# The last layer's second product from float16 pairs, normalised ahead of the transposes

## The chip, the cores and the metric

The kernel runs on one core of one Trainium2 chip. The time of a run is the device time of that core in microseconds (us), and a kernel's time is the median of its runs. Inside the core five engines work beside each other, each through its own instructions in order: TensorE (PE in the profile, its weight loads PEld), VectorE (DVE), ScalarE (ACT), GpSimd (POOL) and SyncE (SP), which issues most of the DMAs. They wait for one another by semaphores.

## The reference, cut to what matters

Three layers follow one another on 2 x 768 = 1536 tokens of 512 features: a clustered attention, a mixture of eight experts of which each token takes one, and a feed-forward layer. The change lies in the last one (and in one load of the second):

```python
h = x @ w_in                                   # 1536x512 by 512x1024
h_max = np.max(h, axis=-1, keepdims=True)
e = np.exp(h - h_max)
sm = e / (np.sum(e, axis=-1, keepdims=True) + 1e-09)
solu = h * sm
mu = np.mean(solu, axis=-1, keepdims=True)
var = np.mean((solu - mu) ** 2, axis=-1, keepdims=True)
ln = (solu - mu) / np.sqrt(var + 1e-06) * g_ln
return (ln @ w_out).astype(np.float32)         # 1536x1024 by 1024x512
```

## The kernel before, in words

**Order of the work.** The order of all instructions is written out by hand. The attention follows the list FLAT. The experts and the preparation of the last layer's weights follow the list MOE (lines 96 to 118), whose steps have a letter and numbers: N and X read an expert's number and load its rows (X.3 those of place 3), W loads its weights, C and Q split a weight chunk (the difference on VectorE or on GpSimd), T transposes the rows, G and H are the expert's first and second product, S stores; P, J and R load and narrow the chunks of w_in (0 to 7) and w_out (8 to 15), K splits a chunk of w_in, M (`m2_gain`, line 1241) multiplies a chunk of w_out by g_ln on ScalarE. There are eight places, one for each expert, in order of their size. An engine works its own steps in the order of the list, so a step that waits holds up what stands behind it on that engine.

**Pairs.** A float32 product is made of three products of rounded values: each operand is split into a high part (rounded by ScalarE) and a low part (the difference, by VectorE or GpSimd), and `mm3` (lines 1036 to 1040) multiplies high by high, high by low and low by high into one PSUM bank. The parts are of type float32r.

**The last layer.** It goes by 12 tiles of 128 tokens, in a loop of 15 iterations (the last lines of `body`). In iteration t TensorE has the first product of tile t (`l_h`, 24 products of 512 columns), the eight transposes of tile t-2 (`l_trans`, line 1362) and the second product of tile t-3 (`l_out`, 24 products of 512 columns into the bank pf), in this order. `l_soft(t)` is the softmax part on VectorE and ScalarE: two maxima (line 1329), a one-column step that joins them (line 1330), two exponentials (line 1334), and u, the product of h and the exponentials (line 1340). `l_norm(t)` makes the mean and the variance of u with two statistics instructions and one that joins them (lines 1348 and 1349), subtracts the mean from u (line 1350, 1024 columns) and has GpSimd make the reciprocal deviation in five one-column steps (lines 1352 to 1356, the last a power). `l_norm(t-1)` stands inside `l_soft(t)`, ahead of u(t). The reciprocal deviation is used only when the finished tile leaves PSUM (line 1376). `l_trans` copies the transposed tile out of the PSUM tile pc, of which there is one, into the pair c: the high part by ScalarE (line 1364), the low part by VectorE (line 1365). GpSimd also makes the low parts of the x tiles from tile 2 on (`l_split`, line 1055) and, in iterations 0 to 2, behind the softmax, the low parts of w_out's eight chunks (line 1033); it issues the scatter of each finished tile (line 701).

That there is one transposed tile at a time, and two finished ones, is said here:

```python
ps_c = ctx.enter_context(tc.tile_pool(name="ps_c", bufs=1, space=PSUM))
ps_f = ctx.enter_context(tc.tile_pool(name="ps_f", bufs=2, space=PSUM))
```

Of the kernel before, what the change touches and what calls it, by code (L numbers as in the profile page):

```python
# [38 lines left out]
NWK = 15  # L39
# [62 lines left out]
W.2.5 C.2.5 W.2.6 G.2.2 E.9 G.2.1 C.2.10 H.2.0 N.3 C.2.9 W.2.7 R.7.0 C.2.8 H.2.1 X.3 P.9 C.2.14 W.3.0 G.2.3 R.7.1  # L102
# [11 lines left out]
X.7 G.6.1 C.6.11 Q.6.10 G.6.3 H.6.0 Q.6.12 W.7.1 Q.6.13 G.6.4 H.6.1 C.6.15 C.7.3 H.6.2 T.7.0 C.6.14 T.7.3 G.6.6 C.7.0  # L114
C.7.1 H.6.3 G.6.5 H.6.4 W.7.2 W.7.3 T.7.2 K.6 T.7.1 G.6.7 Z H.6.5 C.7.7 C.7.4 G.7.0 C.7.5 K.1 C.7.2 M.13 H.6.6 H.6.7
W.7.4 W.7.5 S.6 Q.7.6 M.9 G.7.1 K.0 Q.7.8 Q.7.9 G.7.2 O W.7.6 W.7.7 K.2 Q.7.15 C.7.10 M.12 H.7.0 H.7.1 H.7.2 M.8 G.7.3
C.7.13 Q.7.11 C.7.12 G.7.4 C.7.14 M.11 G.7.5 H.7.3 G.7.6 K.3 K.4 H.7.4 G.7.7 M.14 K.7 M.10 H.7.5 H.7.6 M.15 K.5 H.7.7
# [11 lines left out]
def body(ctx, tc, i, o):  # L129
# [895 lines left out]

    wk = ctx.enter_context(tc.tile_pool(name="wk", bufs=NWK))
# [212 lines left out]

    def m2_gain(c):  # L1240
        nc.scalar.activation(m2n[:, c, :], m2n[:, c, :], AF.Copy, scale=gln[:, c - 8 : c - 7])
# [10 lines left out]
    def last_banks():  # L1252
# [9 lines left out]
        "S": lambda k: wins[k].store(), "P": prep_load, "J": lambda c: prep_load(c, nc.gpsimd), "R": narrow, "E": lambda j: LATE[j](), "K": m2_split, "M": m2_gain,  # L1262
# [58 lines left out]
    def l_soft(t):  # L1321
# [15 lines left out]
        if 0 < t < T - 1:  # L1337
            l_norm(t - 1)
        for half in range(2):
            nc.vector.scalar_tensor_tensor(out=u[:, half], in0=h[:, half], scalar=sc, in1=e[:, half], op0=ALU.mult, op1=ALU.mult)  # L1340
        if t == T - 1:
            l_norm(t)

    def l_norm(t):
# [5 lines left out]
        nc.vector.tensor_scalar(u, u, sm[:, 4:5], None, op0=ALU.subtract)  # L1350

# [6 lines left out]
    def l_trans(t):  # L1358
# [4 lines left out]
        c = z["c"] = l2.tile([128, 2, 1024], F32R, tag="c2", name=f"c2_{t}")  # L1363
        nc.scalar.activation(c[:, 0], pc_, AF.Copy)
        nc.vector.tensor_tensor(out=c[:, 1], in0=pc_, in1=c[:, 0].bitcast(F32), op=ALU.subtract)  # L1365

    def l_out(t):
# [3 lines left out]
        for f in range(NF):  # L1371
            w = m2[8 + f]
            fs = slice(f * 128, f * 128 + 128)
            mm3(po, (c[:, 0, fs], c[:, 1, fs]), (w[:, 0], w[:, 1]), f == 0, f == NF - 1)
        ob = l2.tile([128, 512], F32, tag="ob", name=f"ob_{t}")
        nc.scalar.activation(ob, po, AF.Copy, scale=z["sm"][:, 6:7])
# [3 lines left out]
    for t in range(T + 3):  # L1380
        if 0 < t < T:
            l_h(t)
# [88 lines left out]
```

## Time and profile before

| | us |
|---|---|
| median of 3 runs (lowest, highest) | 582.01 (581.5, 583.67) |
| the profiled execution, its own time | 579.94 |
| its span, from the first to the last instruction | 578.1 |
| TensorE busy in the span | 547.7 (95%) |
| VectorE busy | 403.9 (70%) |
| ScalarE busy | 296.5 (51%) |
| GpSimd busy | 256.9 (44%) |

The granted clock of TensorE is 0.996 of full speed (2.4 GHz) in the mean of the span. Busy shares are averages over stages with different limits, and a busy TensorE is counted with the modelled ends of its products, so it is read by the starts of its instructions: the distance from one start to the next is what a product costs. In a timeline a row stands for one or several instructions of one line (the count behind x), with its start and its duration in front; the brackets at the end tell how long the engine idled before it and what ended that. A duration holds what the instruction waits for once it was begun.

### The profile page before, as it was taken

The numbers are of one execution on the slowest core, as the hardware profiler recorded it, in microseconds if no ns is written. First come the engines' busy times: TensorE is split into PE (matmuls) and PEld (weight loads), VectorE is DVE, ScalarE is ACT, GpSimd is POOL, SyncE is SP. The second block draws the span as 40 slices with busy tenths as digits, with TensorE's granted clock in tenths as the row PEclk, the third lists the DMA queues.
The fourth block names the chain that finished last, engine by engine and source line by source line (L and its number), as shares of the span: only waits on it lengthen the run. The fifth ranks groups of instructions, "written<-read, shape, count | busy, mean of one in ns | idle before, by whom it ended". The sixth has DMA issues, their size and how long they took to land. (4 is left out here: it accounts for less than half of the span.)

```text
span 578.1 us, 12327 instructions
## 1 busy us (share of the span) xinstructions
PE 547.7 (95%) x4652; PEld 469.4 (81%) x4654; DVE 403.9 (70%) x811; ACT 296.5 (51%) x635; POOL 256.9 (44%) x283
## 2 busy tenths in 40 slices
PE   6898899999999999899999999999999999999995
PEld 3676678777778877799999998989988788888884
DVE  6788888787988787748585699877547655544550
ACT  5765776766666565232232468677546424232230
POOL 7467777888675993410000101221307723333221
PEclk9999999999999998999999999999999999999999
DMA  7248468647332110999939577774000000001000
GB/s 256 83 113 261 122 176 255 177 112 226 74 84 59 42 53 19 322 339 394 382 125 385 163 254 252 218 249 152 33 3 2 18 19 18 19 18 39 18 37 36
DMA packets 28866, 81.06 MB, mean 140 GB/s; under 512 B 5356, under 2 KB 5868, under 8 KB 28804
## 3 DMA queue, kind: packets, MB, share of 16 engines
q1 hardware_dynamic: 26020, 70.80, 38.4%
q0 software_dynamic: 2784, 9.44, 4.5%
q8 instruction: 38, 0.62, 0.4%
q14 instruction: 24, 0.20, 0.1%
HBM read 56.17 MB, written 11.53 MB: 117 GB/s over the span
## 5 line engine op out<-in xcount | busy, mean ns | idle before, releaser
L556 POOL TENSOR_TENSOR pl<-pe 128x768 f16<-128x768 f32 (+1 forms) x97 | 128.8, 1347 | 54.6 <-ACT pe L548 48.3
L548 ACT ACTIVATE pe<-pS 128x384 f32<-128x384 f32 x192 | 89.4, 490 | 62.2 <-PE pS L539 54.9
L485 DVE TENSOR_REDUCE ohb<-pm 128x1 bf16<-128x768 f32 x77 | 73.4, 954 | 23.6 <-PE pm L483 23.3
L538 PE MATMUL pS<-w 81*128 81x384 f32 (+1 forms) x192 | 76.8, 400 | 1.9 <-ACT w L508 1.2
L539 PE MATMUL pS<-w 128*128 128x384 f32 x192 | 67.0, 349 | 0.0
L572 PE MATMUL pa<-v,pe 128*128 128x65 f16 x576 | 64.7, 196 | 0.0
L572 PEld LDWEIGHTS <-pe 128*128 128x128 bf16 x576 | 52.9, 98 | 13.9 <-issue 13.4
L573 PE MATMUL pa<-v,pe 128*128 128x64 f16 x576 | 64.0, 195 | 0.0
L574 PE MATMUL pa<-v,pl 128*128 128x65 f16 x576 | 63.7, 193 | 0.0
L573 PEld LDWEIGHTS <-pe 128*128 128x128 bf16 x576 | 54.0, 99 | 0.2
L574 PEld LDWEIGHTS <-pl 128*128 128x128 f16 x576 | 53.9, 99 | 0.0
L1033 POOL TENSOR_TENSOR wk<-rw,wk 128x512 fp32r<-128x512 f32 x13 | 17.7, 1369 | 72.7 <-ACT wk L1032 65.0
L483 PE MATMUL pm<-w 80*128 80x512 f32 (+1 forms) x154 | 43.8, 366 | 5.6 <-DVE ohb L485 3.2
L1334 ACT ACTIVATE e<-h,sm,smeta 128x512 f32<-128x512 f32 x24 | 18.5, 774 | 56.6 <-DVE sm L1330 56.6
L1329 DVE TENSOR_REDUCE sm<-h 128x1 f32<-128x512 f32 x24 | 15.4, 684 | 44.4 <-PE h L1040 41.5
L538 PEld LDWEIGHTS pS<-w 81*128 81x128 f32 (+1 forms) x192 | 37.6, 196 | 8.8 <-ACT pe L548 3.1
L1033 DVE TENSOR_TENSOR wk<-rw,wk 128x512 fp32r<-128x512 f32 x49 | 36.4, 761 | 7.4 <-ACT wk L1032 7.1
L1032 ACT ACTIVATE wk<-rw 128x512 fp32r<-128x512 f32 x62 | 36.7, 630 | 9.1 <-DMA rw<-in_w_dram 7.1
L1038 PE MATMUL pf<-m,c 128*128 128x512 f32 x96 | 38.8, 404 | 0.0
L539 PEld LDWEIGHTS pS<-w 128*128 128x128 f32 x192 | 38.1, 198 | 0.0
L1038 PE MATMUL h<-m,x 128*128 128x512 f32 x96 | 37.7, 392 | 0.4 <-PEq L1294 0.4
L1039 PE MATMUL pf<-m,c 128*128 128x512 f32 x96 | 37.9, 395 | 0.0
(290 smaller groups left out, 1448.9 us busy)
## 6 DMA issues: line engine op xcount, KB each, us to landing
rw<-in_w_dram SPq DMA_DIRECT2D x31, 512.0 KB, 4.4
wk<-in_w_dram SPq DMA_DIRECT2D x25, 512.0 KB, 8.0
w<-w SPq DMA_DIRECT2D x42, 192.0 KB, 4.0
xs_d<-zrow SPq DMA_DIRECT2D x8, 512.0 KB, 5.3
w_w<-in_w_dram SPq DMA_DIRECT2D x8, 512.0 KB, 7.0
raw<-in_qT_dram SPq DMA_DIRECT2D x8, 384.0 KB, 3.8
raw<-in_kT_dram SPq DMA_DIRECT2D x8, 384.0 KB, 4.8
vraw<-in_v_dram SPq DMA_DIRECT2D x8, 384.0 KB, 5.8
```

Source lines behind the costliest of these rows:

```text
L483: nc.tensor.matmul(pm[:, c0:c1], w[0:80, M0 + h, 0, t * 128 : t * 128 + 128], w[0:80, M0 + h, 1, c0:c1], start=True, stop=True)
L485: nc.vector.tensor_reduce(out=s["oh"][:, t, 0, h, C : C + 1], in_=pm, op=ALU.max, axis=AX.X)
L538: nc.tensor.matmul(pS, w[0:kr, M0 + h, 1, ts], w[0:kr, M0 + h, 0, c0:c1], start=b0 == 0, stop=False, skip_group_check=True)
L539: nc.tensor.matmul(pS, w[:, B0 + h, 1, ts], w[:, B0 + h, 0, c0:c1], start=False, stop=True, skip_group_check=True)
L548: nc.scalar.activation(pe[:, e0 - b0 : e0 + n], s["bank"][:, : kb * n], AF.Exp, scale=0.125)
L556: eng.tensor_tensor(out=pl, in0=pe, in1=ph, op=ALU.subtract)
L572: nc.tensor.matmul(pa[:, o0 : o0 + D + 1], ph[:, qs], vh, start=(t == 0 and qt == q0), stop=False, skip_group_check=True)
L573: nc.tensor.matmul(pa[:, o0 : o0 + D], ph[:, qs], vl, start=False, stop=False, skip_group_check=True)
L574: nc.tensor.matmul(pa[:, o0 : o0 + D + 1], pl[:, qs], vh, start=False, stop=(t == NT - 1), skip_group_check=True)
L1033: (eng or nc.vector).tensor_tensor(out=t[:, 1, :], in0=rw, in1=t[:, 0, :].bitcast(F32), op=ALU.subtract)
L1038: nc.tensor.matmul(out, a[0], b[0], start=first, stop=False, skip_group_check=True)
L1039: nc.tensor.matmul(out, a[0], b[1], start=False, stop=False, skip_group_check=True)
```

## The change

The second product of the last layer takes its operands as pairs of float16 in place of float32r (`out_split` and the new lines of `l_trans`). For that w_out times g_ln is scaled by a power of two that the chip finds: eight maxima (the new steps B on VectorE), two small steps that join them (Y, the second with a float32 product of 128 columns on TensorE), and the gain M now multiplies by g_ln times that scale and so stands behind Y in the list. The transposed activations are multiplied by 512, and what leaves PSUM by one constant (`osc`). The reciprocal deviation moves from there to the activations: `l_apply` subtracts the mean and multiplies by it, ahead of the transposes, and takes the place of the subtraction in `l_norm`. `l_norm(0)` moves to the end of `l_soft(0)`; `l_apply(t-1)` stands behind u(t), for tile 0 ahead of u(1). The splits of w_out's chunks 8 to 13 move ahead of the softmaxes of tiles 0 and 1. And X.3 stands two steps of SP's earlier, ahead of W.2.7.

```diff
-W.2.5 C.2.5 W.2.6 G.2.2 E.9 G.2.1 C.2.10 H.2.0 N.3 C.2.9 W.2.7 R.7.0 C.2.8 H.2.1 X.3 P.9 C.2.14 W.3.0 G.2.3 R.7.1
+W.2.5 C.2.5 W.2.6 G.2.2 E.9 G.2.1 C.2.10 H.2.0 N.3 X.3 C.2.9 W.2.7 R.7.0 C.2.8 H.2.1 P.9 C.2.14 W.3.0 G.2.3 R.7.1
...
-X.7 G.6.1 C.6.11 Q.6.10 G.6.3 H.6.0 Q.6.12 W.7.1 Q.6.13 G.6.4 H.6.1 C.6.15 C.7.3 H.6.2 T.7.0 C.6.14 T.7.3 G.6.6 C.7.0
-C.7.1 H.6.3 G.6.5 H.6.4 W.7.2 W.7.3 T.7.2 K.6 T.7.1 G.6.7 Z H.6.5 C.7.7 C.7.4 G.7.0 C.7.5 K.1 C.7.2 M.13 H.6.6 H.6.7
-W.7.4 W.7.5 S.6 Q.7.6 M.9 G.7.1 K.0 Q.7.8 Q.7.9 G.7.2 O W.7.6 W.7.7 K.2 Q.7.15 C.7.10 M.12 H.7.0 H.7.1 H.7.2 M.8 G.7.3
-C.7.13 Q.7.11 C.7.12 G.7.4 C.7.14 M.11 G.7.5 H.7.3 G.7.6 K.3 K.4 H.7.4 G.7.7 M.14 K.7 M.10 H.7.5 H.7.6 M.15 K.5 H.7.7
+X.7 G.6.1 C.6.11 Q.6.10 G.6.3 B.8 H.6.0 Q.6.12 W.7.1 Q.6.13 G.6.4 H.6.1 C.6.15 B.9 C.7.3 H.6.2 T.7.0 C.6.14 T.7.3
+G.6.6 C.7.0 B.10 C.7.1 H.6.3 G.6.5 H.6.4 W.7.2 W.7.3 T.7.2 B.11 K.6 T.7.1 G.6.7 Z H.6.5 C.7.7 C.7.4 B.12 G.7.0 C.7.5
+K.1 C.7.2 H.6.6 H.6.7 B.13 W.7.4 W.7.5 S.6 Q.7.6 G.7.1 K.0 B.14 Q.7.8 Q.7.9 G.7.2 O W.7.6 W.7.7 K.2 B.15 Q.7.15 C.7.10
+Y.0 H.7.0 H.7.1 H.7.2 G.7.3 C.7.13 Y.1 Q.7.11 C.7.12 M.13 G.7.4 C.7.14 M.9 G.7.5 H.7.3 M.12 G.7.6 K.3 M.8 K.4 H.7.4
+M.11 G.7.7 K.7 M.14 H.7.5 H.7.6 M.10 M.15 K.5 H.7.7
...
+    am2 = kp.tile([128, NF + 3], F32, name="am2")
+    gsc = kp.tile([128, NF], F32, name="gsc")
+    osc = am2[:, NF + 1 : NF + 3]
+
+    def m2_max(c):
+        nc.vector.tensor_reduce(out=am2[:, c - 8 : c - 7], in_=m2n[:, c, :], op=ALU.max, axis=AX.X, apply_absolute_value=True)
+
+    def m2_scale(part):
+        m = am2[:, NF : NF + 1]
+        if part == 0:
+            nc.vector.tensor_tensor(out=am2[:, :NF], in0=gln, in1=am2[:, :NF], op=ALU.mult)
+            nc.vector.tensor_reduce(out=m, in_=am2[:, :NF], op=ALU.max, axis=AX.X, apply_absolute_value=True)
+            return
+        px = PL.ps_t.tile([128, 512], F32, tag="pt", name="pt_scale")
+        nc.tensor.matmul(px[:, :128], m.to_broadcast([128, 128]), identf, start=True, stop=True)
+        nc.vector.tensor_reduce(out=osc[:, 0:1], in_=px[:, :128], op=ALU.max, axis=AX.X)
+        nc.vector.tensor_scalar(osc[:, 0:1], osc[:, 0:1], 2.0 ** -90, None, op0=ALU.max)
+        nc.vector.tensor_scalar(bits(osc[:, 0:1]), bits(osc[:, 0:1]), 0x7F800000, None, op0=ALU.bitwise_and)
+        nc.vector.tensor_scalar(bits(osc[:, 1:2]), bits(osc[:, 0:1]), -1.0, float(268 << 23), op0=ALU.mult, op1=ALU.add)
+        nc.vector.tensor_scalar(gsc, gln, osc[:, 1:2], None, op0=ALU.mult)
+        nc.vector.tensor_scalar(bits(osc[:, 0:1]), bits(osc[:, 0:1]), 1.0, float(-23 << 23), op0=ALU.mult, op1=ALU.add)
+
     def m2_gain(c):
-        nc.scalar.activation(m2n[:, c, :], m2n[:, c, :], AF.Copy, scale=gln[:, c - 8 : c - 7])
+        nc.scalar.activation(m2n[:, c, :], m2n[:, c, :], AF.Copy, scale=gsc[:, c - 8 : c - 7])
+
+    def out_split(c, pool):
+        t = pool.tile([128, 2, 512], F32R, tag="wk", name=f"m2_{c}")
+        hi, lo = (t[:, j].bitcast(F16)[:, :512] for j in range(2))
+        nc.scalar.activation(hi, m2n[:, c, :], AF.Copy)
+        nc.gpsimd.tensor_tensor(out=lo, in0=m2n[:, c, :], in1=hi, op=ALU.subtract)
+        m2[c] = (hi, lo)
...
-        if 0 < t < T - 1:
+        if t == 1:
+            l_apply(0)
+        elif 0 < t < T - 1:
             l_norm(t - 1)
         for half in range(2):
             nc.vector.scalar_tensor_tensor(out=u[:, half], in0=h[:, half], scalar=sc, in1=e[:, half], op0=ALU.mult, op1=ALU.mult)
+        if t == 0:
+            l_norm(0)
+        elif 1 < t < T - 1:
+            l_apply(t - 1)
         if t == T - 1:
             l_norm(t)
+            l_apply(t)
+
+    def l_apply(t):
+        sm, u = ts_[t]["sm"], ts_[t]["u"]
+        nc.vector.tensor_scalar(u, u, sm[:, 4:5], sm[:, 6:7], op0=ALU.subtract, op1=ALU.mult)
...
         nc.vector.bn_aggr(out=sm[:, 4:6], in_=bs)
-        nc.vector.tensor_scalar(u, u, sm[:, 4:5], None, op0=ALU.subtract)
...
-        c = z["c"] = l2.tile([128, 2, 1024], F32R, tag="c2", name=f"c2_{t}")
-        nc.scalar.activation(c[:, 0], pc_, AF.Copy)
-        nc.vector.tensor_tensor(out=c[:, 1], in0=pc_, in1=c[:, 0].bitcast(F32), op=ALU.subtract)
+        c = z["c"] = l2.tile([128, 2, 1024], F16, tag="c2", name=f"c2_{t}")
+        nc.scalar.activation(c[:, 0], pc_, AF.Copy, scale=512.0)
+        nc.vector.scalar_tensor_tensor(out=c[:, 1], in0=pc_, scalar=512.0, in1=c[:, 0], op0=ALU.mult, op1=ALU.subtract)
...
-            mm3(po, (c[:, 0, fs], c[:, 1, fs]), (w[:, 0], w[:, 1]), f == 0, f == NF - 1)
+            mm3(po, (c[:, 0, fs], c[:, 1, fs]), w, f == 0, f == NF - 1)
...
-        nc.scalar.activation(ob, po, AF.Copy, scale=z["sm"][:, 6:7])
+        nc.scalar.activation(ob, po, AF.Copy, scale=osc[:, 0:1])
...
+        if t < 2:
+            for c in range(8 + 3 * t, 11 + 3 * t):
+                out_split(c, wk if c < NWK else lw2)
         if t < T - 1:
             l_soft(t)
-        if t < 3:
-            for c in range(8 + 3 * t, min(11 + 3 * t, 16)):
-                m2_split(c, wk if c < NWK else lw2, nc.gpsimd)
+        if t == 2:
+            for c in range(14, 16):
+                out_split(c, wk if c < NWK else lw2)
         if t == T - 1:
             l_norm(t - 1)
+            l_apply(t - 1)
```


## Rows read from the trace of the kernel before

**Rows 1.** Stages: us, busy time (instructions) of each engine, clock, DMA share, GB/s.

```profile
380.00:420.00 40.00, 40.00 (x259) 37.58 (x258) 27.36 (x45) 25.74 (x55) 10.78 (x8) 1.00 0.39 123
```

**Rows 2.** Timeline of TensorE, 554 to 561 us: start us, us, what, [idle before].

```profile
554.30 0.48 PE L1038 MATMUL pf<-m,c 128*128 128x512 f32 x1
...
554.62 0.39 PE L1039 MATMUL pf<-m,c 128*128 128x512 f32 x1
...
559.97 1.03 PE L1362 MATMUL pc<-cst,u 128*128 128x128 f32 x8
```

**Rows 3.** Timeline of TensorE's weight loads, 449 to 453 us.

```profile
451.48 0.85 PEld L1362 LDWEIGHTS pc<-cst,u 128*128 128x128 f32 x8 [1.81 <-DVE c L1365]
```

**Rows 4.** Timeline of TensorE, 36.4 to 36.8 us.

```profile
36.45 0.38 PE L902 MATMUL pS<-warmb,onesb 128*128 128x512 bf16 x1
...
36.66 0.19 PE L572 MATMUL pa<-v,pe 128*128 128x65 f16 x1
```

**Rows 5.** Timeline of TensorE, 102.4 to 103.1 us.

```profile
102.45 0.19 PE L572 MATMUL pa<-v,pe 128*128 128x65 f16 x1
...
103.00 0.42 PE L538 MATMUL pS<-w 81*128 81x384 f32 x1
```

**Rows 6.** Timeline of VectorE, 432 to 452 us.

```profile
433.85 0.22 DVE L1330 SCALAR_TENSOR_TENSOR sm<-sm,smeta 128x1 f32<-128x1 f32 x1
...
435.82 1.41 DVE L1340 SCALAR_TENSOR_TENSOR u<-h,smeta,e 128x512 f32<-128x512 f32 x2 [1.75 <-ACT e L1334]
...
438.36 1.29 DVE L1329 TENSOR_REDUCE sm<-h 128x1 f32<-128x512 f32 x2 [1.13 <-PE h L1040]
...
447.42 1.56 DVE L1350 TENSOR_SCALAR u<-u,sm 128x1024 f32<-128x1024 f32 x1
```

**Rows 7.** Timeline of ScalarE, 398 to 478 us.

```profile
423.02 1.33 ACT L1241 ACTIVATE w_w<-w_w,gln 128x512 f32<-128x512 f32 x2
```

**Rows 8.** Timeline of TensorE's weight loads, 297 to 299 us.

```profile
297.81 0.30 PEld L1085 LDWEIGHTS pt<-cst,xs 128*128 128x128 f32 x2
```

**Rows 9.** Timeline of VectorE, 553 to 558 us.

```profile
554.94 1.27 DVE L1348 BATCH_NORM_STATS2 bs<-u 128x6 f32<-128x512 f32 x2
...
556.25 0.21 DVE L1349 BATCH_NORM_AGGREGATE sm<-bs 128x2 f32<-128x12 f32 x1
...
556.49 0.75 DVE L1350 TENSOR_SCALAR u<-u,sm 128x1024 f32<-128x1024 f32 x1
...
557.16 1.22 DVE L1365 TENSOR_TENSOR c<-pc,c 128x1024 fp32r<-128x1024 f32 x1
```

**Rows 10.** Timeline of GpSimd, 428 to 452 us.

```profile
429.84 1.29 POOL L1055 TENSOR_TENSOR x<-x2T,x 128x512 fp32r<-128x512 f32 x1 [15.94 <-ACT x L1052]
...
447.15 1.29 POOL L1055 TENSOR_TENSOR x<-x2T,x 128x512 fp32r<-128x512 f32 x1
```

**Rows 11.** Groups by shape, VectorE, 400 to 578 us: count, busy us, mean ns.

```profile
L1350 DVE TENSOR_SCALAR u<-u,sm 128x1024 f32<-128x1024 f32 x12 | 9.9, 826 | 0.4
...
L1330 DVE SCALAR_TENSOR_TENSOR sm<-sm,smeta 128x1 f32<-128x1 f32 x12 | 3.7, 306 | 0.4
```

**Rows 12.** Groups by shape, whole span, GpSimd, VectorE and weight loads.

```profile
L556 POOL TENSOR_TENSOR pl<-pe 128x768 f16<-128x768 f32 x68 | 104.3, 1551 | 27.4 <-ACT pe L548 25.0 <-PE pm L483 2.2
...
L556 POOL TENSOR_TENSOR pl<-pe 128x384 f16<-128x384 f32 x29 | 24.7, 868 | 27.2 <-ACT pe L548 23.3 <-DVE r L579 3.9
...
L890 DVE TENSOR_SCALAR x2T<-cst,enum,posf 128x128 f32<-128x128 f32 x6 | 1.7, 354 | 0.0
...
L574 PEld LDWEIGHTS <-pl 128*128 128x128 f16 x576 | 53.9, 99 | 0.0
```

**Rows 13.** Timeline of GpSimd, 543 to 560 us.

```profile
544.88 0.19 POOL L1355 TENSOR_TENSOR sm<-sm 128x1 f32<-128x1 f32 x1
...
545.15 0.57 POOL L1356 TENSOR_TENSOR sm<-sm,cst 128x1 f32<-128x1 f32 x1
...
556.60 0.69 POOL L1355 TENSOR_TENSOR sm<-sm 128x1 f32<-128x1 f32 x1 [2.19 <-DVE sm L1349]
```

More of the change, by code (lines that the diff above doesn't have):

```diff
@@ L1024, in __init__ @@
             self.ps_h = pool("ps_h", nph, space=PSUM)
+    kp = ctx.enter_context(tc.tile_pool(name="kp", bufs=1))
     wk = ctx.enter_context(tc.tile_pool(name="wk", bufs=NWK))
@@ L1261, in body @@
         "H": lambda k, f: wins[k].g2(f), "X": lambda k: wins[k].load_x(), "T": lambda k, d: wins[k].trans_x(d),
-        "S": lambda k: wins[k].store(), "P": prep_load, "J": lambda c: prep_load(c, nc.gpsimd), "R": narrow, "E": lambda j: LATE[j](), "K": m2_split, "M": m2_gain,
+        "S": lambda k: wins[k].store(), "P": prep_load, "J": lambda c: prep_load(c, nc.gpsimd), "R": narrow, "E": lambda j: LATE[j](), "K": m2_split, "M": m2_gain, "B": m2_max, "Y": m2_scale,
         "O": last_banks,
```

## The prediction

> **The bound.** I read the stages first, then the last layer's TensorE timeline, then who waited in it. In the stage before the last layer TensorE is busy for all of its 40.00 us, so work added to its queue there is paid in full; Vector is busy for 27.36 us of them and ScalarE for 25.74 us, so 12.6 us and 14.3 us are free [rows 1]. The last layer is a chain of token tiles; at its end the 24 products of one tile's second product start at 554.30 us and the next transposes at 559.97 us: 5.67 us, 236 ns a product, without a gap [rows 2]. The first product of a tile takes 320 ns to the next start, 90 ns more than the others. The only place in that layer where TensorE waited for another engine is its beginning: 1.81 us ahead of tile 1's transposes, for Vector's copy of tile 0 out of the PSUM tile that both use [rows 3]. So TensorE's queue sets the end, with one hole that Vector and GpSimd make.
>
> **Part 1**, the second product in float16 pairs (removes time). The count stays, 12 tiles of 24 products of 512 columns; only the column type changes. No 512-column float16 product is in the trace. The nearest row is a 512-column bfloat16 product that is followed 0.21 us later by a float16 one [rows 4]. Eighteen float16 products of 65, 64 and 65 columns take 102.45 to 103.00 us, 30.6 ns each for 64.7 columns: at one column per cycle of 2.4 GHz that is 26.9 ns and 3.6 ns more, which for 512 columns makes 213.3 + 3.6 = 217 ns [rows 5]. Bounds: 210 ns, and no gain at all (236 ns); I take 216 ns, since both rows are near it. A tile then costs 24 x 0.216 + 0.09 = 5.27 us in place of 5.67 (5.665 unrounded), 0.395 us less, and 12 tiles give -4.7 us.
> The Trainium skill speaks against this figure: its page "TensorE: Matmul & The Clock Gate", section "Back-to-back issue gap", puts a stream of weight load and 512-column product pairs at about 131 ns each. By that the term would be some 30 us; the two rows above, at 210 to 217 ns, don't bear it out.
>
> **Part 2**, the scale of w_out (adds). Eight maxima of 512 columns on Vector: a 512-column maximum takes 0.65 us (1.29 for two [rows 6]), 5.2 us together, inside the 12.6 us that Vector has free; if that cover went, the one that is late holds an eviction back by 0.65 us. The eight gain copies on ScalarE keep their number, two take 1.33 us [rows 7], and move behind the scale, into its 14.3 free us; without that cover one gain, 0.7 us, would stand ahead of an eviction. Neither is charged. The scale's matrix product goes into TensorE's full queue: eight float32 transposes of 128 columns take 1.03 us, 0.13 each [rows 2]; I charge two of them, +0.25 us, with 0 and 0.6 as bounds (the latter if Vector's six small instructions are behind).
>
> **Part 3**, place 3's rows. The two loads move ahead of one weight load in SP's queue. Place 3's first transposes, at 297.81 us, waited for nothing [rows 8], so they gain nothing; the weight load that is passed is issued two DMAs later, under 1 us, and belongs to the end of place 2's second product, which comes after these transposes. 0; if it were late, 1 us.
>
> **Part 4**, the beginning of the last layer (moves and adds waits). Six of the float16 splits of w_out go ahead of the softmaxes of tiles 0 and 1; tile 0's statistics go ahead of tile 1's maximum; and the normalisation now takes the reciprocal deviation, which comes from GpSimd, so Vector waits for GpSimd where it did not. What is queued behind that wait on Vector is c(0), the copy for which TensorE waited. Vector also waits for GpSimd in a second way: the 1024-wide subtraction that takes 0.75 us [rows 9] took 1.56 us at 447.42 [rows 6] while GpSimd's 512-wide subtraction ran from 447.15 to 448.44 [rows 10]; it ended 0.54 us after it. Likewise the little combining step behind the maxima takes 0.22 us alone [rows 6] and 306 ns in the mean of 12. By the means of both groups [rows 11], 12 x 0.086 + 12 x 0.073, such stalls cost 1.9 us now.
> A float16 split on GpSimd: 868 ns for 384 columns and 1551 for 768 [rows 12], so 1.08 us for 512, against 1.29 us for today's float32 subtraction [rows 10]; I take 1.08 and keep 1.29 as a bound. Laid out in order, with GpSimd starting at 429.84 us as now [rows 10]: splits 8 to 10 until 433.1, tile 2's x split until 434.4. Tile 0's maxima end at 433.8, the combining step is held until 434.5, u(0) starts 1.75 us later [rows 6] and ends at 437.7, the statistics (1.27 and 0.21 us [rows 9]) at 439.1. Tile 1's maxima run 439.15 to 440.45 (today from 438.36, after 1.13 us of idling that the statistics now fill [rows 6]). GpSimd ends tile 0's deviation at 440.1 and starts split 11; the combining step is held until 441.35; tile 0's normalisation waits for split 12 and ends at 442.85, in time for its transposes. u(1) waits for its exponentials until 443.1 and ends at 444.5; tile 2's maxima end at 445.8; tile 4's x split holds the combining step until 446.65; u(2) runs 448.4 to 449.8; split 14 holds tile 1's normalisation, which ends at 450.75; c(0) ends at 452.0, where today TensorE goes on at 451.48 [rows 3]. +0.55 us, with bounds of -1.0 (nothing held by GpSimd) and +1.8 (splits of 1.29 us, which also bring tile 3's x split late).
>
> **Part 5**, the steady tiles. The normalisation of tile t-1 now comes after u(t), and the copy c(t-2) after it; both are needed only behind the next tile's first product, which has 24 products too, so some 5 us later by [rows 2]. That hides them; without it, what they are late would be TensorE's wait. No charge.
>
> **Part 6**, the end. Tile 11's normalisation stands ahead of c(10), and tile 11's transposes need the PSUM tile that c(10) frees. The statistics end at 556.46 [rows 9], 0.06 later with the new c(9) (a scalar_tensor_tensor of 1024 columns: between 1.22 [rows 9] and 1.41, two of 512 [rows 6]; I take 1.28). GpSimd then needs 0.14 to start, 0.19 and 0.57 us with 0.08 between [rows 13]; its 0.69 at 556.60 was the subtraction beside it, which is gone. So 557.5; the normalisation, 0.75 us, until 558.3; c(10) until 559.55; transposes at 559.6. TensorE is there at 559.97 - 2 x 0.395 = 559.18 [rows 2]: +0.4 us, bounds 0 and 1.4 (normalisation at 1.28 us, and 0.69 kept).
> For the normalisation with two per-partition scalars the trace has one row, with a mean of 354 ns for 128 columns [rows 12]. The subtraction that it replaces takes 0.75 us at 1024 columns with one such scalar, and that is one bound. The other takes 0.22 us of the 354 as fixed (the one-column step [rows 6]) and the rest, 1.04 ns a column, for 1024: 1.28 us. I take 0.75, the row of the same width and type. The Trainium skill's page "VectorE: DVE Perf Modes", section "What auto-detection actually checks", asks of a double-rate instruction a single source in SBUF and even sizes, and names no limit on scalars. By that rule it would be 0.75, by the 128-column row at worst 1.28; no run here shows it at 1024.
>
> **Sum.** -4.7 + 0.25 + 0.55 + 0.4 = -3.5 us. The profiled execution took 579.94 us (578.1 of span); it becomes 576.4. The median of the runs shown is 582.01, 2.1 us above that execution; from it the same sum gives 578.5 us.
>
> **Rivals.**
> A: GpSimd doesn't hold Vector up at the beginning, so statistics and earlier splits win: part 4 is -1.0, time 577.0. For it: the statistics fill 1.13 us in which Vector idles today. Against: the 1.56 us row. 0.20.
> B: the beginning gets longer, because the splits take 1.29 us or the normalisation 1.28: part 4 at +1.8, 579.8, and with the end at its bound 580.8. For it: Vector and GpSimd are the ones behind there today. 0.25.
> C, slower: a float16 column costs what the short products show in all, 30.6/64.7 = 0.473 ns, so 512 cost 242 ns. Then a tile is 24 x 0.242 + 0.09 = 5.90 us, 12 tiles +2.8, with the other 1.2 us 586.0. It decides from 232 ns a product upward, where the gain no longer pays the 1.2. Against: the 0.21 us [rows 4]. 0.05.
> D: the type changes nothing for a 512-column product: +1.2, 583.2. Same evidence against. 0.04.
> E: successive float16 pairs overlap, and the pitch falls to the weight load's 99 ns [rows 12]: 288 x 0.137 = 39.5 us, 543.7. 0.01. The Trainium skill's 131 ns (above; page "TensorE: Matmul & The Clock Gate", section "Back-to-back issue gap") is of this kind; [rows 4, 5] speak against it.
>
> **Numbers.** The forecast has 0.45. A measurement of this kernel can tell about 0.5%, 2.9 us, from no change: the border is 579.1. The forecast lies 0.6 us under it, so 0.37 of its 0.45 count as faster; with A and E 0.58. The rest of it, B and D make 0.37 for the same; C 0.05 for slower. The range takes in A with its bounds and B with the end at its bound: 576.0 to 581.2; C, D and E stay out, one in ten, and so do some of the sums of several bounds.
>
> **What shows it.** Right: the pf products start 216 ns apart and a tile's 24 take 5.27 us; the iteration of a steady tile is 0.395 us shorter; tile 1's transposes still wait for c, about 2 us; tile 11's transposes wait for c(10), under 1 us; in the stage before, TensorE stays full. Wrong: a pitch over 230 ns; a wait at h of tile 3 for its x split; waits of TensorE for DVE in the steady tiles; GpSimd splits not near 1.08 us.

## The result and the profile after

Timed beside the kernel before on the same chip, the changed kernel takes 576.72 us (median of 6 runs, 574.13 to 578.63) against 582.69 us (6 runs, 581.5 to 585.76): a ratio of 0.9894, with a 95% interval from 0.9862 to 0.9926, so 4.3 to 8.0 us less. The forecast was 578.5 us, so faster, with a range from 576.0 to 581.2 us that holds the measured time. The profiled execution took 578.63 us, with a span of 576.8 us. The first line of its page is the busy time of each engine; before, it was 547.7 (PE), 403.9 (DVE), 296.5 (ACT) and 256.9 us (POOL):

```profile
PE 544.0 (94%) x4656; PEld 443.7 (77%) x4656; DVE 411.3 (71%) x827; ACT 296.7 (51%) x635; POOL 251.9 (44%) x283
```

VectorE has more to do, TensorE and GpSimd have less; the totals don't tell where, so the stages have to be read.

The two spans differ by only 1.3 us, and the last layer alone explains more than that. It runs from the first start of an h product to the last start of a pf product. These are the two rows of the changed kernel's TensorE timeline (start, duration, instruction):

```profile
429.57 0.39 PE L1040 MATMUL h<-m,x 128*128 128x512 f32 x1
...
570.61 0.38 PE L1042 MATMUL pf<-m,c 128*128 128x512 f16 x1
```

That is 141.04 us. In the kernel before, the same two rows are 145.15 us apart:

```profile
426.63 0.39 PE L1038 MATMUL h<-m,x 128*128 128x512 f32 x1
...
571.78 0.40 PE L1040 MATMUL pf<-m,c 128*128 128x512 f32 x1
```

**The last layer is 4.1 us shorter; what lies ahead of it was 2.9 us longer in this execution.** The experts' first product starts at 249.53 us in place of 247.85, so the attention had 1.7 of the 2.9 us. This is a stage of the attention in the changed kernel (stretch, busy time and instructions of PE, PEld, DVE, ACT and POOL, granted clock, DMA share, GB/s):

```profile
50.00:100.00 50.00, 46.74 (x573) 37.25 (x571) 41.34 (x77) 32.73 (x73) 37.97 (x28) 0.97 0.72 210
```

The granted clock was 0.97 in the mean there. The kernel before was granted 1.00 in that stretch and did 603 products in it in place of 573; its own stretch at 0.97 was the one from 200 to 250 us. The change edits nothing in the attention. The parts ahead of the last layer vary by such amounts from execution to execution (below), which is why the length of the last layer is the measure in what follows: it came out within 0.15 us wherever its code was the same.

The stages around the change in the changed kernel, the first to be read against [rows 1]:

```profile
380.00:420.00 40.00, 40.00 (x257) 37.40 (x257) 34.15 (x64) 25.62 (x57) 10.79 (x8) 1.00 0.46 145
420.00:460.00 40.00, 38.48 (x200) 31.02 (x199) 28.36 (x47) 23.14 (x48) 18.88 (x28) 1.00 0.01 2
460.00:500.00 40.00, 40.00 (x193) 27.50 (x192) 19.67 (x32) 12.46 (x23) 14.03 (x29) 1.00 0.07 27
```

TensorE is still full where the maxima were added; VectorE's 27.36 us became 34.15. Only the middle row, the beginning of the last layer, leaves TensorE idle, by 1.5 us. The steady part of the last layer is TensorE's alone.

**The products.** The answers to [rows 2] in TensorE's timeline are two pf products of one tile and the first h product behind them:

```profile
471.95 0.38 PE L1041 MATMUL pf<-m,c 128*128 128x512 f16 x1
472.17 0.38 PE L1042 MATMUL pf<-m,c 128*128 128x512 f16 x1
472.19 0.58 PE L1040 MATMUL h<-m,x 128*128 128x512 f32 x1
472.61 0.39 PE L1041 MATMUL h<-m,x 128*128 128x512 f32 x1
```

Float16 products start 0.22 us apart (215.8 ns in the mean of those within a tile, against 232.7 ns before). The shown duration of 0.38 us is the pipelined one and says nothing about the cost. The last two rows show a thing to read with care. The first h product is recorded 0.02 us behind the last pf product, with a duration of 0.58 us in place of 0.39, and the second h product starts 0.42 us later. The two steps together are 0.44 us, one float16 step and one float32r step (0.216 and 0.228): nothing is lost there, one start is recorded early. The 0.32 us of the first pf product before [rows 2] are of the same kind. From the start of a steady tile's transposes to its second pf product it was 1.105 us before and is 1.088 now; the difference is that of one step. So a stretch of one kind of product is a poor measure: pf's seems to gain 0.67 us (4.99 in place of 5.665), h's to lose 0.19 (5.67 in place of 5.48) and the transposes' to lose 0.08 (0.87 in place of 0.79). A whole turn is what counts: 11.94 us before, 11.535 after, 0.405 us less, as much as 24 products at 16.9 ns less each.

**The beginning.** TensorE's weight loads, the second row answering to [rows 3], the first one in the h product of tile 3:

```profile
448.24 0.19 PEld L1042 LDWEIGHTS h<-m,x 128*128 128x128 f32 x1 [0.46 <-POOL x L1057]
...
454.72 0.86 PEld L1402 LDWEIGHTS pc<-cst,u 128*128 128x128 f32 x8 [1.62 <-DVE c L1405]
```

A new wait for the x split of tile 3, and the known one for c(0). Counted from the layer's first product, the transposes of tile 1 begin at 454.72 - 429.57 = 25.15 us, against 24.85 before: 0.30 us later. VectorE's timeline there, answering to [rows 6]. L1361 is the little combining step, L1384 the normalisation, L1405 the copy c:

```profile
436.71 0.80 DVE L1361 SCALAR_TENSOR_TENSOR sm<-sm,smeta 128x1 f32<-128x1 f32 x1
...
443.30 0.96 DVE L1361 SCALAR_TENSOR_TENSOR sm<-sm,smeta 128x1 f32<-128x1 f32 x1
444.18 1.74 DVE L1384 TENSOR_SCALAR u<-u,sm 128x1024 f32<-128x1024 f32 x1
...
452.53 1.01 DVE L1384 TENSOR_SCALAR u<-u,sm 128x1024 f32<-128x1024 f32 x1
453.46 1.21 DVE L1405 SCALAR_TENSOR_TENSOR c<-pc,c 128x1024 f16<-128x1024 f32 x1
...
459.20 0.80 DVE L1384 TENSOR_SCALAR u<-u,sm 128x1024 f32<-128x1024 f32 x1
```

GpSimd's timeline of the same stretch, answering to [rows 10], with the float16 splits of w_out (L1271) and the splits of x (L1057):

```profile
432.83 3.41 POOL L1271 TENSOR_TENSOR m<-w_w,m 128x512 f16<-128x512 f32 x3 [16.23 <-ACT m L1270]
436.20 1.30 POOL L1057 TENSOR_TENSOR x<-x2T,x 128x512 fp32r<-128x512 f32 x1
...
443.09 3.87 POOL L1271 TENSOR_TENSOR m<-w_w,m 128x512 f16<-128x512 f32 x3
446.91 2.52 POOL L1057 TENSOR_TENSOR x<-x2T,x 128x512 fp32r<-128x512 f32 x2
...
451.82 2.73 POOL L1271 TENSOR_TENSOR m<-w_w,m 128x512 f16<-128x512 f32 x2
```

A step of VectorE that stands alone takes 0.22 us (combining) or 0.80 us (normalising). Beside a split of GpSimd the same steps take 0.80, 0.96, 1.74 and 1.01 us. The first of these ends at 437.51 us, the x split beside it at 437.50; where the splits were moved and none runs beside that step, it takes 0.22 us (e7_splits_behind below).

**The end.** VectorE's timeline, answering to [rows 9]:

```profile
556.33 0.21 DVE L1391 BATCH_NORM_AGGREGATE sm<-bs 128x2 f32<-128x12 f32 x1
557.53 0.81 DVE L1384 TENSOR_SCALAR u<-u,sm 128x1024 f32<-128x1024 f32 x1 [0.99 <-POOL spacer L701]
558.26 1.22 DVE L1405 SCALAR_TENSOR_TENSOR c<-pc,c 128x1024 f16<-128x1024 f32 x1
```

GpSimd's, answering to [rows 13]:

```profile
556.68 0.19 POOL L1395 TENSOR_TENSOR sm<-sm 128x1 f32<-128x1 f32 x1 [2.19 <-DVE sm L1391]
556.95 0.55 POOL L1396 TENSOR_TENSOR sm<-sm,cst 128x1 f32<-128x1 f32 x1
```

And TensorE's, from the first pf product of tile 9 to the transposes of tile 11:

```profile
554.00 0.38 PE L1040 MATMUL pf<-m,c 128*128 128x512 f16 x1
...
559.53 1.09 PE L1402 MATMUL pc<-cst,u 128*128 128x128 f32 x8 [0.19 <-DVE c L1405]
```

This is the new wait that the forecast named: statistics, deviation on GpSimd, normalisation, c(10), then the transposes. They start 5.53 us behind the first pf product, where 24 products take 5.18: 0.35 us late, of which the modelled end of the last product leaves 0.19 to be seen as idle.

### The profile page after: what moved, and what is told of

It reads as the page before. It is cut to its first block, busy times and chain, and to the rows that moved or that the text cites. A ratio compares the mean times of both kernels' runs of the same rounds, so it can differ in the third digit from the quotient of the medians.

```text
span 576.8 us, 12355 instructions
## 1 busy us (share of the span) xinstructions
PE 544.0 (94%) x4656; PEld 443.7 (77%) x4656; DVE 411.3 (71%) x827; ACT 296.7 (51%) x635; POOL 251.9 (44%) x283
## 3 DMA queue, kind: packets, MB, share of 16 engines
HBM read 56.17 MB, written 11.53 MB: 117 GB/s over the span
## 5 line engine op out<-in xcount | busy, mean ns | idle before, releaser
L1034 ACT ACTIVATE wk<-rw 128x512 fp32r<-128x512 f32 x62 | 36.8, 630 | 11.4 <-DMA rw<-in_w_dram 8.8
L1040 PE MATMUL h<-m,x 128*128 128x512 f32 x96 | 39.2, 408 | 0.3 <-PEq L1325 0.3
L1042 PE MATMUL h<-m,x 128*128 128x512 f32 x96 | 37.7, 392 | 0.0
L1041 PE MATMUL h<-m,x 128*128 128x512 f32 x96 | 37.4, 389 | 0.0
```

The costliest lines, as they stand in the source:

```text
L1040: nc.tensor.matmul(out, a[0], b[0], start=first, stop=False, skip_group_check=True)
L1041: nc.tensor.matmul(out, a[0], b[1], start=False, stop=False, skip_group_check=True)
L1042: nc.tensor.matmul(out, a[1], b[0], start=False, stop=last, skip_group_check=True)
```

## The experiments

Ten more kernels ran. The table has the starts of the last layer's first h and last pf product in the profiled execution, their distance, the median time, and the ratio on record to the kernel before on the same chip, which is not simply the quotient of two medians.

| kernel | first h to last pf, us | last layer, us | median, us | ratio [95% interval] |
|---|---|---|---|---|
| before | 426.63 to 571.78 | 145.15 | 581.15 to 582.86, by chip | 1 |
| changed | 429.57 to 570.61 | 141.04 | 576.72 | 0.9894 [0.9862, 0.9926] |
| float32r pairs again (e1_type_back) | 428.14 to 574.27 | 146.13 | 583.39 | 1.003 [1.0001, 1.0059] |
| no scale (e2_no_scale) | 428.84 to 569.81 | 140.97 | 576.96 | 0.9906 [0.987, 0.9941] |
| before, X.3 moved (e3_x3_only) | 429.06 to 574.33 | 145.27 | 582.75 | 1.0018 [0.9992, 1.0044] |
| changed, X.3 in its old place (e4_x3_back) | 426.44 to 567.46 | 141.02 | 577.44 | 0.9925 [0.9895, 0.9955] |
| c(10) first (e5_tail) | 431.02 to 571.57 | 140.55 | 578.09 | 0.9899 [0.9868, 0.993] |
| transposes a turn later (e6_trans_later) | 427.92 to 567.50 | 139.58 | 574.95 | 0.9863 [0.9831, 0.9895] |
| splits behind (e7_splits_behind) | 425.45 to 570.11 | 144.66 | 581.13 | 0.9962 [0.9939, 0.9984] |
| e6 and e7 together (e8_later_behind) | 430.39 to 569.71 | 139.32 | 576.86 | 0.9881 [0.9846, 0.9915] |
| e5, e6 and e7 together (e9_all_moves) | 424.23 to 562.99 | 138.76 | 574.51 | 0.9902 [0.9868, 0.9936] |
| e9 with h from float16 pairs too (e10_h_f16) | 426.59 to 562.21 | 135.62 | 570.77 | 0.9832 [0.9795, 0.9869] |

The layer's start scatters from 424.23 to 431.02 us among kernels that hardly differ ahead of it, and the intervals of the ratios reach about 0.3%, some 2 us, to either side, so a median alone settles little below that.

### The type by itself

The theory: the product's type carries all of the gain, and the rest of the change costs about a microsecond. The rival: order and normalisation gain by themselves.

```diff
-        hi, lo = (t[:, j].bitcast(F16)[:, :512] for j in range(2))
+        hi, lo = t[:, 0], t[:, 1]
...
-        c = z["c"] = l2.tile([128, 2, 1024], F16, tag="c2", name=f"c2_{t}")
+        c = z["c"] = l2.tile([128, 2, 1024], F32R, tag="c2", name=f"c2_{t}")
```

> The changed kernel with its pairs of type float32r again; scale, order, normalisation and place 3's rows stay changed. Theory (the float16 type is the whole gain): a tile's 24 products of the second product are 236 ns apart again in place of 216, so the last layer, from the start of its first product to the start of its last, takes 145.1 to 146.2 us (141.04 with the change, 145.14 before), TensorE no longer waits ahead of tile 11's transposes, and the time is 0 to 1.5 us above the kernel before. Rival (scale, order or place 3's rows bring part of it): the time stays 2 us or more under the kernel before.

The pitch of the pf products is 232.3 ns again, and the last layer takes 146.13 us, 1.0 us more than before the change and 5.1 more than with float16. The ratio, 1.003, lies above 1. So what else was changed costs about a microsecond in the last layer, and the type pays for it. The beginning depends on the type too. This run's timeline of weight loads has the wait for c(0):

```profile
454.17 0.85 PEld L1402 LDWEIGHTS pc<-cst,u 128*128 128x128 f32 x8 [1.75 <-DVE c L1405]
```

And its timeline of GpSimd has the first three splits of w_out:

```profile
431.40 3.78 POOL L1271 TENSOR_TENSOR m<-w_w,m 128x512 fp32r<-128x512 f32 x3 [16.23 <-ACT m L1270]
```

These float32r splits take 3.78 us, 1.26 each; three float16 splits took 3.41, 1.14 each. The weight load of tile 1's transposes starts 26.03 us behind the layer's first product (454.17 less 428.14), against 25.15 with float16 and 24.85 before. At the end, TensorE waits for nothing here: with the longer products it comes to tile 11's transposes later, when c(10) is done.

### The scale by itself

```diff
-X.7 G.6.1 C.6.11 Q.6.10 G.6.3 B.8 H.6.0 Q.6.12 W.7.1 Q.6.13 G.6.4 H.6.1 C.6.15 B.9 C.7.3 H.6.2 T.7.0 C.6.14 T.7.3
+X.7 G.6.1 C.6.11 Q.6.10 G.6.3 H.6.0 Q.6.12 W.7.1 Q.6.13 G.6.4 H.6.1 C.6.15 C.7.3 H.6.2 T.7.0 C.6.14 T.7.3
...
-        nc.scalar.activation(m2n[:, c, :], m2n[:, c, :], AF.Copy, scale=gsc[:, c - 8 : c - 7])
+        nc.scalar.activation(m2n[:, c, :], m2n[:, c, :], AF.Copy, scale=gln[:, c - 8 : c - 7])
...
-        nc.scalar.activation(ob, po, AF.Copy, scale=osc[:, 0:1])
+        nc.scalar.activation(ob, po, AF.Copy, scale=1.0 / 512)
```

> The changed kernel without the search for the scale: the eight maxima and the two small steps are left out, the gain multiplies by g_ln alone and what leaves PSUM by 1/512. Theory: 0.2 to 0.3 us less than the changed kernel, all of it ahead of the last layer, whose length stays 141.0 us. Rival (the maxima on Vector hold TensorE up in the experts' stage, which is 1.25 us longer in the changed profile): 1 us or more less.

576.96 us, and the last layer keeps its length. From the experts' first product to the last layer's first it took 180.34 us in this profile, 180.04 in the changed kernel's and 178.79 in the kernel before. Over all twelve profiles that part lies between 176.6 and 180.7 us, with both kinds of kernel spread over it. The scale's cost is below what these runs can show.

### Place 3's rows by themselves

```diff
-W.2.5 C.2.5 W.2.6 G.2.2 E.9 G.2.1 C.2.10 H.2.0 N.3 C.2.9 W.2.7 R.7.0 C.2.8 H.2.1 X.3 P.9 C.2.14 W.3.0 G.2.3 R.7.1
+W.2.5 C.2.5 W.2.6 G.2.2 E.9 G.2.1 C.2.10 H.2.0 N.3 X.3 C.2.9 W.2.7 R.7.0 C.2.8 H.2.1 P.9 C.2.14 W.3.0 G.2.3 R.7.1
```

> The kernel before with nothing but the load of place 3's rows moved ahead in SP's queue. Theory: no difference, within 0.2% of the kernel before. Rival (the timed runs moved by 6 us where the last layer explains 4): 1.5 to 2 us faster.

> The changed kernel with place 3's rows asked for where they were. Theory: as the changed kernel, 3.9 us (0.7%) under the kernel before, last layer 141.0 us. Rival: 1.5 to 2 us of the gain are gone.

The first is the kernel before with this edit, the second the changed kernel with the edit taken back. Neither moves: 1.0018 with an interval across 1, and 0.9925 beside 0.9894. TensorE's waits for rows of the experts (transposes of xs, waiting for their DMA) were 1.0 us in the kernel before and 1.2 in the changed one; with the edit alone they were 3.4 and without it 1.6 us, so they go their own way from run to run.

### The end: c(10) ahead of the normalisation

```diff
             l_norm(t)
-            l_apply(t)
...
             l_trans(t - 2)
+        if t == T:
+            l_apply(T - 1)
```

> Edit: the normalisation of tile 11 stands on VectorE behind c(10) instead of ahead of it. Theory (the forecast's Part 6): the first weight load of the transposes of tile 11 waits for c(10) by 0.6 to 0.7 us, because c(10) stands behind the normalisation of tile 11, which is held beside a GpSimd span of 1.5 us. With c(10) first that wait goes to 0.2 us or less, the last layer (from its first product to the start of its last) shortens from 141.0 to about 140.5 us, and the time by 0.5 us, which the clocked runs alone would not resolve. Rival: the normalisation itself is then late for the transposes, the wait moves from c(10) to it, and the last layer keeps 141.0 us.

The rows of VectorE show the order exchanged, c at 557.84 us and the normalisation behind it:

```profile
557.71 0.21 DVE L1390 BATCH_NORM_AGGREGATE sm<-bs 128x2 f32<-128x12 f32 x1
557.84 1.17 DVE L1404 SCALAR_TENSOR_TENSOR c<-pc,c 128x1024 f16<-128x1024 f32 x1
558.92 0.80 DVE L1383 TENSOR_SCALAR u<-u,sm 128x1024 f32<-128x1024 f32 x1
```

c now fills the time in which VectorE waited 0.99 us for the deviation, and the normalisation still ends ahead of the transposes. The last layer takes 140.55 us, 0.5 less, as the theory has it; the wait at tile 11 is gone. The expectation has the normalisation held beside GpSimd's span of 1.5 us; it wasn't, since it took 0.81 us beside that span and 0.80 alone. It was late because the deviation was. The medians (578.09 beside 576.72) don't resolve it.

### Transposes a turn later

```diff
-        u = z["u"] = l2.tile([128, 2, 512], F32, tag="u2", bufs=3, name=f"u2_{t}")
+        u = z["u"] = l2.tile([128, 2, 512], F32, tag="u2", bufs=4, name=f"u2_{t}")
...
-        if 2 <= t < T + 2:
-            l_trans(t - 2)
+        if t == 2 or 4 <= t < T + 3:
+            l_trans(0 if t == 2 else t - 3)
...
-        if t >= 3:
-            l_out(t - 3)
+        if t >= 4:
+            l_out(t - 4)
```

> Edit: from tile 1 on every tile's transposes, and every second product, come one turn of the loop later, with a fourth buffer for the tile that waits; nothing is computed differently. Theory: what is left of the change's price is only that the transposes are asked for too early. At the beginning PE waits 1.6 us for c(0) and the transposes of tile 1, at the end 0.6 us; with a turn more, both waits go, the last layer shortens from 141.0 to between 138.9 and 139.3 us and the time stands at 0.985 to 0.989 of the kernel before. Rival: the wait at the beginning is only moved (third tile's h product then waits for its x halves and the softmaxes), the last layer stays above 140.5 us.

139.58 us: the mechanism holds, the size was 0.3 us too large. The expectation added up waits of the weight loads (1.6 and 0.7 us), which overlap the products that are still running; TensorE itself had idled for 1.2 and 0.2 us. What is left here: x of tile 3 (0.46 us) and, at tile 10, a wait of 0.2 us for c(9), which the same order of normalisation and copy makes.

### The splits of w_out back behind the softmaxes

```diff
-        if t < 2:
-            for c in range(8 + 3 * t, 11 + 3 * t):
-                out_split(c, wk if c < NWK else lw2)
         if t < T - 1:
             l_soft(t)
-        if t == 2:
-            for c in range(14, 16):
+        if t < 3:
+            for c in range(8 + 3 * t, min(11 + 3 * t, 16)):
                 out_split(c, wk if c < NWK else lw2)
```

> Edit: the splits of w_out of chunks 8 to 13 stand again behind the softmax of their turn, as before the change. Theory (the forecast's Part 4): the GpSimd halves of the splits hold the two-input steps of VectorE that run beside them, so where they stand sets how long the wait for c(0) is; moved behind the softmax they hold other steps (the statistics, c(0)), x of tile 3 is no longer late (its wait of 0.5 us goes), and the first transposes' wait changes by less than 0.5 us either way: the last layer between 140.3 and 141.5 us. Rival A: the place of the splits was needed, the high parts come later on ScalarE and the low parts later on GpSimd than the first second product asks for them, TensorE waits for them and the last layer is longer than 142 us. Rival B: nothing holds VectorE, and all rows stay as in the changed kernel.

144.66 us, 3 us above the theory's range, and neither the theory nor a rival had the reason. The length is rival A's, but TensorE doesn't wait for a weight, it waits for c(0) still. VectorE's timeline in this kernel, first tile 0's combining step:

```profile
432.62 0.22 DVE L1361 SCALAR_TENSOR_TENSOR sm<-sm,smeta 128x1 f32<-128x1 f32 x1
...
449.79 1.63 DVE L1384 TENSOR_SCALAR u<-u,sm 128x1024 f32<-128x1024 f32 x1 [1.97 <-POOL sm L1396]
451.34 1.21 DVE L1405 SCALAR_TENSOR_TENSOR c<-pc,c 128x1024 f16<-128x1024 f32 x1
```

And GpSimd's:

```profile
443.46 3.43 POOL L1271 TENSOR_TENSOR m<-w_w,m 128x512 f16<-128x512 f32 x3
446.84 1.31 POOL L1057 TENSOR_TENSOR x<-x2T,x 128x512 fp32r<-128x512 f32 x1
448.10 0.21 POOL L1392 TENSOR_TENSOR sm<-sm 128x1 f32<-128x1 f32 x1
...
449.20 0.55 POOL L1396 TENSOR_TENSOR sm<-sm,cst 128x1 f32<-128x1 f32 x1
```

The statistics of tile 1 were done at 446.1 us, but GpSimd's five small steps stand in its queue behind three splits and an x split, 4.7 us of them. The normalisation waits for the deviation, and c(0) stands behind the normalisation. With that, TensorE's timeline:

```profile
452.61 1.09 PE L1402 MATMUL pc<-cst,u 128*128 128x128 f32 x8 [3.74 <-DVE c L1405]
453.54 0.54 PE L1040 MATMUL pf<-m,c 128*128 128x512 f16 x1
453.87 0.63 PE L1041 MATMUL pf<-m,c 128*128 128x512 f16 x1
454.30 0.63 PE L1042 MATMUL pf<-m,c 128*128 128x512 f16 x1
```

And the stretches around it (columns as above, the granted clock third from the end):

```profile
450.00:452.00 2.00, 0.00 (x0) 0.00 (x0) 2.00 (x2) 0.00 (x0) 2.00 (x2) 1.00 0.00 0
452.00:454.00 2.00, 1.39 (x10) 1.15 (x11) 1.97 (x5) 0.00 (x0) 1.91 (x4) 0.91 0.00 0
454.00:457.00 3.00, 3.00 (x9) 1.04 (x8) 2.65 (x6) 2.54 (x5) 1.06 (x5) 0.50 0.00 0
457.00:460.00 3.00, 3.00 (x16) 1.29 (x15) 2.02 (x3) 0.00 (x0) 0.00 (x0) 0.99 0.00 0
```

TensorE idled 3.74 us, and from then on the granted clock went to 0.50, the lower level of 1.2 GHz, for some 3 us. The float16 products start 0.43 us apart in it, in place of 0.216. Eight of them pay 0.21 us each, 1.7 us. So this place costs twice: 2.0 us for the later start of the transposes (27.16 in place of 25.15 us behind the layer's first product) and 1.7 us at half clock, together about the 3.6 us. In the changed kernel, where the idle time was 1.2 us, no product there was slower.

### Moves together, and h from float16 pairs

> Edit: both, the transposes one turn later and the splits of w_out behind the softmaxes. Theory: with a turn more the splits have room, the wait for x of tile 3 (0.5 us) goes as well as the waits for c(0) and c(10), and the last layer is 138.4 to 138.9 us, the shortest of these four; the time stands at 0.984 to 0.988 of the kernel before. Rival: the splits come late for the first second product even so, and the last layer is longer than that of the kernel with the later transposes alone.

With the transposes a turn later the splits behind the softmaxes do no harm, and x of tile 3 is no longer late: 139.32 us, 0.3 less than with the later transposes alone. The theory expected 138.4 to 138.9, having added the 0.46 us to an estimate that was already too large.

The next kernel adds the order of the end, `l_apply(T - 1)` behind `l_trans` in the turn in which it stands, as above:

> Edit: transposes one turn later, splits of w_out behind the softmaxes, and the normalisation of tile 11 behind the c of the turn in which it stands: all three moves together. Theory: what is left in the last layer are the two waits at its end (TensorE 0.2 us, the load queue 0.7 us in the kernel with the later transposes); they go, and the last layer is 138.8 to 139.1 us against 139.3 without the third move. Rival: the normalisation of tile 11 is now what the last transposes wait for, and the length stays at 139.3 us or grows.

138.76 us: in the last layer TensorE waits for no other engine any more, and 2.3 us are gone against the changed kernel. Its median, 574.51 us, has the ratio 0.9902; the difference to the changed kernel's is within both intervals.

The last one takes the type to the first product:

```diff
-        a = ts_[t]["x"][:, :, ds_]
+        a = ts_[t]["x"].bitcast(F16)[:, :, :, :128][:, :, ds_]
...
-        m2[c] = split_chunk(m2n[:, c, :], f"m2_{c}", pool, eng=eng)
+        hi, lo = (t[:, j].bitcast(F16)[:, :512] for j in range(2))
+        nc.scalar.activation(hi, m2n[:, c, :], AF.Copy)
+        (eng or nc.vector).tensor_tensor(out=lo, in0=m2n[:, c, :], in1=hi, op=ALU.subtract)
+        m2[c] = (hi, lo)
...
+            nc.vector.tensor_scalar(smeta, smeta, 2.0 ** -10, None, op0=ALU.mult)
...
-            nc.scalar.activation(x2T[:, :half, bass.ds(self.colreg, self.cap)], b[:, :half], AF.Copy)
+            nc.scalar.activation(x2T[:, :half, bass.ds(self.colreg, self.cap)], b[:, :half], AF.Copy, scale=1024.0)
```

> Edit: the kernel with all three moves, and the first product of the last layer from float16 pairs as well (x times 1024 as it leaves the accumulators, the scale of a token divided by 1024; w_in without a factor). Theory: the type sets the pitch of a product, whichever product it is: the 24 products of a first product go from about 5.66 us, first to last and on, to 24 x 216 ns = 5.2 us, eleven tiles and the first one give 4.5 to 5.5 us, and the last layer is 133.5 to 134.8 us, the time 0.977 to 0.984 of the kernel before. Rival A: VectorE, busy 34.15 of 40 us at turns of 11.54 us, becomes the bound at turns of 11.05 us, waits of TensorE for it come back in every turn, and the last layer stays above 136.5 us. Rival B: the shorter pitch was the second product's own (its operands, its place), the first keeps 227 ns, and nothing is gained.

TensorE's timeline of a steady tile in it:

```profile
476.43 0.38 PE L1042 MATMUL h<-m,x 128*128 128x512 f16 x1
476.65 0.38 PE L1043 MATMUL h<-m,x 128*128 128x512 f16 x1
476.86 1.04 PE L1406 MATMUL pc<-cst,u 128*128 128x128 f32 x8
477.74 0.38 PE L1041 MATMUL pf<-m,c 128*128 128x512 f16 x1
```

135.62 us, 3.1 less. Both rivals fell: the h products start 216 ns apart too (228 before), and no wait for VectorE came back to the layer (one of 0.6 us for an x split did). Rival A had no ground in any case: its 34.15 of 40 us are VectorE's in the experts' stage, and in the steady last layer VectorE is busy for 19.67 of 40 (above). The size was overrated again: the theory took the 5.66 us from the first h to the transposes as the cost of 24 products, but the first h start is recorded 0.2 us early, and 24 products at 0.228 us are 5.47. A turn went from 11.53 to 48 x 0.216 and 0.87 us, 11.23. This kernel is the fastest of all: 570.77 us, 0.9832 of the kernel before, the interval ending at 0.9869.

## Why the prediction was right

The last layer, term by term:

| | predicted, us | measured, us |
|---|---|---|
| part 1, the products of twelve tiles | -4.7 | -4.75 |
| part 4, the beginning | +0.55 | +0.30 |
| part 6, the end | +0.4 | +0.35 |
| the last layer | -3.75 | -4.10 |

**Part 1** stood on two far rows, one of bfloat16 and one of 65 columns [rows 4, 5], and its pitch came out within a nanosecond: 216 taken, 215.8 measured, and 0.405 us a turn for 0.395. That such rows carry over to 512 float16 columns wasn't known ahead; e10_h_f16 shows the same pitch at another product. One sign failed as it was written: a tile's 24 products take 4.99 us and not 5.27, because the start that is recorded early is now the first h product's (by 0.19 us) and no longer the first pf product's (by 0.09). So the slow first product of 0.09 us was a matter of the record as well; it stood on both sides of the difference, so the sum didn't suffer. Two borders did: the 236 ns that the forecast takes as no gain have the 0.09 us in them, which its formula adds once more. No gain begins at 232 ns, and by its own formula rival C decides from 228 ns on, not from 232. The entry of -4.75 is what remains of -4.10 after the two others; 288 products at 16.9 ns less make 4.87, and where the 0.1 us between them went was not found. The Trainium skill, page "TensorE: Matmul & The Clock Gate", section "Back-to-back issue gap", has about 131 ns for a pair of weight load and 512-column product. Measured are 215.8 ns, and the measurement decides: rival E is out. Rivals C and D fell with the same rows; the kernel with float32r pairs is rival D on the chip, its last layer 1.0 us longer than before the change, where the rival's sum was 1.2.

**Part 2.** TensorE stayed full in the stage where the maxima came in, and VectorE was 6.8 us busier there, as the cover required. The scale's product stands among products of the expert (ph) in TensorE's timeline:

```profile
413.36 0.31 PE L1042 MATMUL ph<-xTm,wk 128*128 128x320 f32 x1
413.51 0.38 PE L1256 MATMUL pt_scale<-cst,am 128*128 128x128 f32 x2
...
413.88 0.31 PE L1041 MATMUL ph<-xTm,wk 128*128 128x320 f32 x1
```

From the first of these rows to the last are two steps of ph, which take 0.29 us elsewhere in that group and 0.52 here. The scale's product thus took about 0.22 us of the queue, with no wait, and the charge was 0.25. The runs without the scale can't resolve so little.

**Part 3** was charged with nothing, and two kernels show no difference clear of the noise.

**Part 4.** The order that was laid out instruction by instruction held. Shifted by the 2.94 us by which the layer starts later, the forecast's ends and the measured ones are: combining step of tile 0 437.4 and 437.5, its statistics 442.0 and 442.1, combining step of tile 1 444.3 and 444.3, normalisation of tile 0 445.8 and 445.9, normalisation of tile 1 453.7 and 453.5, c(0) 454.9 and 454.7. The holding of VectorE beside GpSimd's splits is thus the right mechanism, against rival A, and e7_splits_behind shows it from the other side: without a split beside it tile 0's combining step took 0.22 us. Half of rival B came true, and with it a sign that the forecast had named for being wrong: x of tile 3 was late (0.46 us). The splits took 1.14 us; the forecast had 1.08, where its two rows [rows 12] give 1.10, and 1.29 as a bound. That wait is inside the +0.30, since the transposes wait for c(0) in any case. The size was 0.25 us off, mostly in the last two rows, where the normalisation was held less long than laid out.

**Part 6.** The forecast had the deviation at 557.5 us, c(10) done at 559.55 and the transposes at 559.6. It counted from the end of tile 11's statistics, 556.46 us there and 556.54 here, so the times can be laid side by side: they came at 557.5, 559.48 and 559.53. For the normalisation with two per-partition scalars the bounds were 0.75 and 1.28 us; alone it takes 0.80 to 0.81. The Trainium skill, page "VectorE: DVE Perf Modes", section "What auto-detection actually checks", names no limit on scalars; the measured 0.80 us at 1024 columns agrees with it. That the order of the two steps makes the wait is what e5_tail shows.

**The total.** Against the 582.01 us of the forecast's runs its 578.5 stood for 3.5 us less; the last layer gives 4.1, and the medians of six runs each differ by 6.0. More runs settle most of that: on the chip of the first four experiments the 29 runs of the kernel before have a mean of 581.1 us, and the 18 runs of the two kernels with the changed kernel's last layer (e2_no_scale and e4_x3_back) a mean of 576.8, so 4.3 us less, with a standard error of 0.6. The last layer is enough to explain that. The first comparison's interval, 4.3 to 8.0 us, just misses its 4.1; nothing in the profiles accounts for more, and six runs to a side are few.

## What to carry to other kernels

Where TensorE's queue is the bound, count a type's gain from start to start over a whole turn, because the start of a group's first product can be recorded early, here by 0.1 to 0.2 us, which moves time from one group to another in the record alone. Ask what is waited for by the engine itself, not by its load queue, before summing up what a wait is worth. And a small step in an in-order queue is as late as the bulk work ahead of it: GpSimd's five one-column steps, and VectorE's copy behind the step that needs them, set when TensorE went on; a turn of slack, for which a fourth buffer was needed, or an exchange of two instructions took these waits away.

## What was not expected

- After 3.74 us without a product TensorE's granted clock was 0.50 for some 3 us, and a late copy cost 3.6 us where its own lateness was 2.0.
- The first float32r product behind float16 products is recorded 0.02 us behind the last of them and 0.42 us ahead of the next. It looks like a slow step and costs nothing that a turn shows.
- GpSimd's indirect DMA took 1.55 us at 557.71 beside the normalisation and 0.96 us at 560.39, when VectorE was idle; whether the normalisation was the cause was not tried.
- A mean clock of 0.97 over 50 us is one stretch of some 3 us at 0.50: from 218 us on in the kernel before, from 69 us on in the changed one. Seven of the twelve profiles have one at 217 to 221 us, and those of e7_splits_behind, e9_all_moves and e10_h_f16 have none ahead of the last layer. How much of the scatter there comes from them was not settled: the experts' first product starts at 246.9 us with one of them (e4_x3_back) and at 248.9 with none (e7_splits_behind).
